# Two-layer attention and feed-forward decode step with gradients: order of the last pass's end, its last weight gradient and its last stores

## Chip, cores and metric

The kernel runs on one NeuronCore of a Trainium2 chip. The metric is the device time of one execution in microseconds; lower is better. The kernel before took 2014.3 us in the median of 8 runs (2004.38 to 2015.78).

## What is computed

One token passes twice through the same attention and feed-forward weights. The outputs are the result and the gradients of all inputs, among them those of the whole K and V caches (4 key/value heads, 65536 positions, 128 wide, 64 MB each in bf16), which are used by both layers, so that their gradients are sums over two layers.

```python
def _A_ref(x, k_cache, v_cache, wq, wo):          # 32 query heads, 4 key/value heads
    q = (x @ wq) ...
    scores = jnp.einsum("bhqd,bhkd->bhqk", q, k) * (Dh ** -0.5)
    p = _softmax(scores, axis=-1)
    o = jnp.einsum("bhqk,bhkd->bhqd", p, v)
    return o ... @ wo
...
x = x + _A_ref(_layernorm(x), A_k_cache, A_v_cache, A_wq, A_wo)
x = x + _B_ref(_layernorm(x), B_w1, B_b1, B_w2, B_b2)     # relu, squared
x = x + _A_ref(_layernorm(x), A_k_cache, A_v_cache, A_wq, A_wo)
x = x + _B_ref(_layernorm(x), B_w1, B_b1, B_w2, B_b2)
...
_out, _vjp = jax.vjp(_f, A_x, A_k_cache, A_v_cache, A_wq, A_wo, B_w1, B_b1, B_w2, B_b2)
_grads = _vjp(grad_out)
```

## The kernel before

The caches are streamed four times: two forward passes (one a layer), a backward pass for the second layer, and a last pass, `attn_bwd4` (L1192), that finishes the first layer's backward and writes the gradients dK and dV of both layers. K and V come in blocks of 1 MB (`J` = 32 columns of 128 positions); a group is one of the four key/value heads and has 16 blocks of each. In the last pass the groups run from 3 down to 0 and the blocks of a group from 15 down to 0, so group 0's block 0 is the last.

An item is a quarter of a block (8 columns). `pipeline` (L795) walks over the items; each stage is a function with a lag, and step i runs it on item i minus the lag:

- `vT` (lag 0): loads the V block where it is new and turns 8 tiles on TensorE (L1249); a copy brings them to SBUF (`kt`).
- `vS` (lag 2): 8 small products into `ps_sc` (L1282), and once a block the VectorE multiplication that makes `X` (L1290), dS of both layers; X is turned into `xt` (L1262).
- `dV8` (lag 3): in the first two quarters of a block, `outer16` (L1295): four matmuls in row pairs into `ps_gg` (L1303) and two copies into a 1 MB staging slot. After the second call GpSimd issues the slot's store (L1309).
- `k8` (lag `B4_LAG` = 7): loads the K block where it is new, 8 matmuls into dQ's sum (`ps_acc`, L1329), and in the last two quarters `outer16` for dK, from the same `xt`. At the end of a group dQ is folded and `on_group` is called.

The copies (`evac`, L139) go to ScalarE (L150) or VectorE (L153), whichever has the smaller planned load.

All 1 MB pieces live in one arena of 20 slots (12, and 8 that hold the probabilities until a group is done). `take_one` (L268) picks a slot by the step in which it was given back: for a load the newest that is 9 steps old, for staging the newest that is 1 step old; a slot with a store counts as given back 5 steps later (`STORE_STEPS`, L67). Loads are issued by SyncE in program order (L331 for K and V, L425 for weights), stores by GpSimd in program order; an instruction waits on semaphores for what was last in its slot, so a late store holds up what comes next into its slot. GpSimd also makes `xin`, a copy of probabilities that X's block needs (L1256).

Between the stages a background list runs the other gradients, a piece a step: the outer products for w1, w2, wo and wq (`g_outer`, L1371), and the products that give dn and dO. A wq gradient of one group is 2 MB: `rows2` (L1345) turns two vectors into rows (`rowb` from dQ, `rowa` from the layer norm's output, twice), `rank2` (L1362) makes eight pieces of 128 x 1024 that are copied, and two stores of 1 MB go out (L1386). The one for the last group runs after the pass:

```python
    attn_bwd4(3, L1, L3, on4, bg, b4, [(12 + B4_LAG, last_v), (12, pre_load("wq4", lambda: wq_slabs(lastg[3], 2))), (5, fill4)])
    bg.drain()
    run(gwq(lastg[3]))
```

The list at the end gives functions with the number of steps before the pass's end in which they run: the last three V loads, the loads of the last wq slabs, and `fill4`, which turns the wq slabs (64 transposes, L637). When the last dQ is folded, `on4` (L1621) runs the product with these slabs (`PRE["rows"].run()`, L669), the layer norm's backward, and stores dx0 (L193). The instructions' order on each engine is that of a list scheduler within the dependencies, not always that of the source.

Of the kernel before, what the change touches and what calls it, by code (L numbers as in the profile page):

```python
# [20 lines left out]
def kernel(  # L21
# [117 lines left out]
    def evac(out, in_, kind="bf"):  # L139
        n = 1  # L140
        for d in in_.shape[1:]:
            n *= d
        ca = 0.17 + n * 0.00083
        cd = 0.13 + n * (0.00105 if kind == "f32" else 0.00054)

        if PS["pass4"] and kind == "bf":
            ca += 1.5
        if kind == "kta" or kind != "kt" and load["act"] + ca <= load["dve"] + cd:
            load["act"] += 0.17 + n * 0.00083
            nc.scalar.copy(out=out, in_=in_)  # L150
        else:
            load["dve"] += cd
            nc.vector.tensor_copy(out=out, in_=in_)  # L153
# [12 lines left out]
    def col_from_dram_f(v1d, n, name):  # L166
        nj = n // P
        rows = tmp.tile([nj // 4, 4 * P], BF, name="rows_f", tag="rows_f", bufs=1)
        nc.sync.dma_start(out=rows[:], in_=v1d.rearrange("(s x) -> s x", x=4 * P))
        pt = ps_mv([P, 4, 8], BF)  # L170
        col = vec.tile([P, nj // 4, 4], F32, name=name)
        for j in range(4):
            nc.tensor.transpose(pt[:, j, 0:nj // 4], f_cols(rows, j), ident_b[0:nj // 4, 0:nj // 4])
            nc.vector.tensor_copy(out=col[:, :, j], in_=pt[:, j, 0:nj // 4])
        return col[:, :, :].rearrange("p s j -> p (s j)")

    def col_to_dram_f(col, n, v1d):
        nj = n // P
        rows = tmp.tile([nj // 4, P, 4], BF, name="rows_f", tag="rows_f", bufs=1)
# [5 lines left out]
        nc.gpsimd.dma_start(out=v1d.rearrange("(s x) -> s x", x=4 * P), in_=rows[:].rearrange("s p j -> s (p j)"))  # L185
# [191 lines left out]
    B4_LAG = TLEAD + J // 8 + 1  # L377
# [814 lines left out]
    def attn_bwd4(p, La, Lb, on_group, bg, stack, end=()):  # L1192
# [16 lines left out]
        def g_setup(g):  # L1209
# [6 lines left out]
            ndt = dspool.tile([64, J, R2], BF, name="ndt4", tag="ndt4", bufs=1)  # L1216
            for i, L in enumerate((La, Lb)):
                nc.vector.tensor_copy(out=ndt[:, :, i * R:(i + 1) * R], in_=L["nd2"][:, sl].unsqueeze(1).to_broadcast([64, J, R]))
# [48 lines left out]
        def vS(g, c8):  # L1267
# [27 lines left out]
        def outer16(name, out, key, xt, gg, j1):  # L1295
# [4 lines left out]
            for m in range(2):  # L1300
# [6 lines left out]
                evac(stg[:, jj:jj + 8, :].rearrange("p j d -> p (j d)"), pg[:, :], kind="f32")  # L1307
            if j1 + 16 == J:
                nc.gpsimd.dma_start(out=out, in_=stg)  # L1309
                state.pop(key).free(stored=True)  # L1310

        def dV8(g, c8):
            b, j0 = divmod(c8, J)
            if 2 * j0 < J:
                outer16("gstv", half(GVv, g, b), "stv", state[("xe", g, b)], state[("GG", g, c8 // SU)][1], 2 * j0)

        def k8(g, c8):
# [3 lines left out]
            X, xt = state[("xd", g, b)]  # L1321
# [40 lines left out]
    def rank2(out, lhs, rhs):  # L1362
# [6 lines left out]
        evac(out, pg[:, 0:n], kind="f32")  # L1369

# [250 lines left out]
    def on4(g):  # L1621
# [54 lines left out]
```

## Time and profile before

| stretch of the profiled execution | length us | TensorE busy | granted clock | DMA share | GB/s |
|---|---|---|---|---|---|
| start of the last pass, 1212 to 1310 | 98.0 | 78.60 | 0.81 | 0.78 | 298 |
| its body, 1310 to 1900 | 590.0 | 494.07 | 0.88 | 1.00 | 411 |
| 1900 to 1940 | 40.0 | 32.65 | 0.91 | 0.98 | 407 |
| 1940 to 1980 | 40.0 | 38.58 | 0.96 | 0.94 | 350 |
| 1980 to the end | 33.5 | 18.26 | 0.73 | 0.43 | 173 |

The profiled execution took 2015.27 us; its span on the core is 2013.5 us. Over the whole span TensorE is busy 80%, VectorE 58%, ScalarE 52%, and 794.97 MB move at 393 to 395 GB/s. Times in the views count from the start of the span. A DMA share of 1.00 means that all 16 DMA engines have packets in work all the time; the busy time of TensorE is modelled and does not mean its peak. In a timeline or a table of groups, the bracket at the end of a row is the idle time of that engine just before, and what ended it.

### The profile page before, as it was taken

The page shows a single profiled execution, that of the slowest core. Times are in us where ns is not written, and L with a number is a line of the kernel's source. Part 1 is how long each engine was busy: PE and PEld are TensorE (multiplying, and loading weights), DVE is VectorE, ACT ScalarE, POOL GpSimd, SP SyncE. Part 2 cuts the span into 40 slices and gives each one's busy share as a digit, 9 for nine tenths or more (in the row PEclk, how much of TensorE's full clock was granted, in tenths as well). Part 3 has the DMA queues.
Part 4 walks back from the last instruction along what each step waited for, and adds up shares of the span by engine and source line. Part 5 has one row for each costly group of instructions (what it writes and reads, how often), then busy time and mean ns, then how long its engine had stood idle before and what let it go on. Part 6 is the DMA issues. An engine that isn't in the chain of part 4 may idle for free. (4 is left out here: it accounts for less than half of the span.)

```text
span 2013.5 us, 67001 instructions
## 1 busy us (share of the span) xinstructions
PE 1607.8 (80%) x30210; PEld 1310.0 (65%) x30210; DVE 1174.5 (58%) x2358; ACT 1043.9 (52%) x1613; POOL 143.4 (7%) x332
## 2 busy tenths in 40 slices
PE   6877788687777786877777887888878878698986
PEld 6877777587777686767777785455545555455554
DVE  5645455255545543545454466677758767678775
ACT  3444344253443353425363455577658667567665
POOL 0000000000000000000000001111112111111211
PEclk9989899799999997998898998789879989889888
DMA  9999999999999998999999986999999999999996
GB/s 389 421 419 419 419 422 404 395 402 419 419 418 420 420 403 298 363 420 420 421 416 410 402 301 256 346 423 424 421 411 414 403 423 383 368 422 425 423 369 241
DMA packets 110845, 794.97 MB, mean 395 GB/s; under 512 B 9424, under 2 KB 9438, under 8 KB 49374
## 3 DMA queue, kind: packets, MB, share of 16 engines
q1 hardware_dynamic: 86510, 624.99, 76.2%
q0 software_dynamic: 24048, 165.70, 19.9%
q8 instruction: 236, 3.87, 0.8%
q14 instruction: 51, 0.42, 0.1%
HBM read 624.96 MB, written 165.69 MB: 393 GB/s over the span
## 5 line engine op out<-in xcount | busy, mean ns | idle before, releaser
L153 DVE COPY kt<-ps_tr 128x1024 bf16<-128x1024 bf16 x724 | 497.6, 689 | 477.0 <-PE ps_tr L936 254.9
L150 ACT CAST arena<-ps_gg 128x1024 bf16<-128x1024 f32 x452 | 440.2, 1010 | 223.3 <-PE ps_gg L1303 172.3
L936 PE MATMUL ps_tr<-ident_b,arena 128*128 128x128 bf16 x3840 | 310.2, 226 | 59.5 <-DMA arena<-in_A_k_cache_dram 39.7
L936 PEld LDWEIGHTS <-arena 128*128 128x128 bf16 x3840 | 234.4, 101 | 64.1 <-DMA arena<-in_A_k_cache_dram 41.1
L153 DVE CAST arena<-ps_gg 128x1024 bf16<-128x1024 f32 (+1 forms) x191 | 228.8, 1198 | 79.1 <-PE ps_gg L1303 40.0
L150 ACT COPY kt<-ps_tr 128x1024 bf16<-128x1024 bf16 x164 | 172.4, 1053 | 192.4 <-PE ps_tr L1128 126.5
L1303 PE MATMUL ps_gg<-GG,xt 64*128 64x512 bf16 x1024 | 214.1, 416 | 43.6 <-DVE arena L153 25.7
L1038 PE MATMUL ps_acc<-arena 128*128 128x64 bf16 (+4 forms) x4096 | 204.3, 195 | 50.6 <-DMA arena<-in_A_v_cache_dram 32.6
L1249 PE MATMUL ps_tr<-ident_b,arena 128*128 128x128 bf16 x1824 | 178.2, 235 | 44.1 <-DMA arena<-in_A_v_cache_dram 43.1
L954 PE MATMUL ps_sc<-L_qpad,kt 128*128 128x64 bf16 (+7 forms) x3584 | 183.6, 194 | 19.5 <-issue 14.3
L1128 PE MATMUL ps_tr<-ident_b,arena 128*128 128x128 bf16 x1920 | 156.2, 227 | 50.4 <-DMA arena<-in_A_v_cache_dram 49.0
L1019 ACT ACTIVATE arena<-S_sb,L_negm 128x128 bf16<-128x128 f32 x256 | 165.6, 1003 | 55.1 <-DVE L_negm L1004 55.1
L1038 PEld LDWEIGHTS <-arena 128*128 128x128 bf16 x4096 | 158.2, 100 | 53.2 <-DMA arena<-in_A_v_cache_dram 35.0
L1249 PEld LDWEIGHTS <-arena 128*128 128x128 bf16 x1824 | 120.4, 105 | 99.1 <-issue 51.6
L954 PEld LDWEIGHTS <-kt 128*128 128x128 bf16 x3584 | 153.2, 100 | 26.4 <-issue 19.7
L1128 PEld LDWEIGHTS <-arena 128*128 128x128 bf16 x1920 | 118.3, 102 | 54.0 <-DMA arena<-in_A_v_cache_dram 52.2
L1329 PE MATMUL ps_acc<-X,arena 128*128 128x64 bf16 (+3 forms) x2048 | 119.5, 198 | 15.7 <-DMA arena<-in_A_k_cache_dram 15.7
L1019 ACT ACTIVATION_READ_ACCUMULATOR arena<-S_sb,L_negm 128x1 f32 x256 | 128.1, 500 | 0.0
L1329 PEld LDWEIGHTS <-arena 128*128 128x128 bf16 x2048 | 86.7, 102 | 51.6 <-issue 34.1
L1282 PE MATMUL ps_sc<-DOB,kt 128*128 128x64 bf16 (+3 forms) x1824 | 118.0, 200 | 0.0
L1282 PEld LDWEIGHTS <-kt 128*128 128x128 bf16 x1824 | 86.0, 103 | 47.9 <-issue 46.4
L1173 PE MATMUL ps_acc<-dsT,arena 128*128 128x64 bf16 (+7 forms) x2048 | 102.8, 194 | 16.8 <-DMA arena<-in_A_k_cache_dram 12.3
(269 smaller groups left out, 2099.9 us busy)
## 6 DMA issues: line engine op xcount, KB each, us to landing
arena<-in_A_k_cache_dram SPq DMA_DIRECT2D x86, 2048.0 KB, 20.7
arena<-in_A_v_cache_dram SPq DMA_DIRECT2D x83, 2048.0 KB, 21.8
out_dram<-arena POOLq DMA_DIRECT2D x151, 1024.0 KB, 11.2
arena<-in_A_v_cache_dram SPq DMA_DIRECT2D x76, 1024.0 KB, 15.2
arena<-in_A_k_cache_dram SPq DMA_DIRECT2D x76, 1024.0 KB, 12.8
arena<-in_B_w_dram SPq DMA_DIRECT2D x32, 896.0 KB, 6.9
arena<-in_A_wq_dram SPq DMA_DIRECT2D x22, 1024.0 KB, 14.0
arena<-in_A_wo_dram SPq DMA_DIRECT2D x18, 1024.0 KB, 15.9
```

The lines of the kernel that those rows point to most:

```text
L150: nc.scalar.copy(out=out, in_=in_)
L153: nc.vector.tensor_copy(out=out, in_=in_)
L936: nc.tensor.transpose(pt[:, i, :], kb8[:, i, :], ident_b[:, :])
L954: nc.tensor.matmul(state["ps_s"][:, s:s + w, :].rearrange("p a b -> p (a b)"), lhsT=kt[:, i, :], rhs=L["qpad"][:, g, 0:w, :].rearrange("p ...
L1019: nc.scalar.activation(out=E(p, g, c0, SU)[:, :, h], in_=S[:, h, :], func=ACTF.Exp, bias=L["negm"][:, g, su, h:h + 1], scale=SCALE, accum_ ...
L1038: nc.tensor.matmul(ps_o[:, 0:w, :], lhsT=vb8[:, i, :], rhs=E(p, g, c, w), start=(c % SU == 0), stop=(c % SU == SU - 1), skip_group_check=True)
L1128: nc.tensor.transpose(pt[:, i, :], vb8[:, i, :], ident_b[:, :])
L1173: nc.tensor.matmul(ps_dq[:, 0:w, :].rearrange("p a b -> p (a b)"), lhsT=kb8[:, i, :], rhs=dsT[:, s:s + w, :].rearrange("p a b -> p (a b)") ...
L1249: nc.tensor.transpose(pt[:, i, :], vb8[:, i, :], ident_b[:, :])
L1282: nc.tensor.matmul(state["ps_dp"][:, s:s + w, :].rearrange("p a b -> p (a b)"), lhsT=vt[:, i, :], rhs=DOB[:, g, 0:w, :].rearrange("p a b - ...
L1303: nc.tensor.matmul(pg[:, 512 * h:512 * h + 512], lhsT=xt[64 * h:64 * h + 64, j1 // 8 + m, :], rhs=gg[64 * h:64 * h + 64, :, :].rearrange(" ...
L1329: nc.tensor.matmul(ps_dq[:, 0:w, :].rearrange("p a b -> p (a b)"), lhsT=kb8[:, i, :], rhs=X[:, s:s + w, :].rearrange("p a b -> p (a b)"), ...
```

## The change

In six parts (a few lines of the helpers `col_from_dram_f` and `col_to_dram_f`, which take the arena slot, are left out of the diff):

- dK gets a stage of its own, `dK8`, at the old lag of 7 (`DK_LAG`); `k8`, now dQ alone, runs four items later (`B4_LAG` = 11), and so K blocks are asked for one block later. X gets a third buffer, the rows `ndt` shrink from 32 copies to one that is broadcast, and `rows_f` becomes an arena slot.
- A finished staging slot is put in a list (`pend`). Its store is issued when the list is longer than `held` allows: nothing is held before item 24 of the last group (of 64), then one, two from item 32, three from item 40. `cap` lets them go 7, 5 and 3 steps before the end.
- Each store also waits for the copy that was recorded last when the store is recorded (`add_manual_dep`).
- The last group's wq gradient, `g_outer_last`: both `rowa` are made in `fill4`, `rowb` as soon as dQ is folded, then one `rank2` after the product for dn and the other seven after the dx0 store; four stores of 0.5 MB.
- The remaining background work is drained in `fill4` rather than after the pass.
- The wq slabs are loaded 20 steps before the pass's end instead of 12, and `fill4` runs 10 steps before it instead of 5; the pass is four steps longer.

```diff
@@
             ca += 1.5
         if kind == "kta" or kind != "kt" and load["act"] + ca <= load["dve"] + cd:
             load["act"] += 0.17 + n * 0.00083
-            nc.scalar.copy(out=out, in_=in_)
-        else:
-            load["dve"] += cd
-            nc.vector.tensor_copy(out=out, in_=in_)
+            return nc.scalar.copy(out=out, in_=in_)
+        load["dve"] += cd
+        return nc.vector.tensor_copy(out=out, in_=in_)
 
 
     def col_from_dram(v1d, n, name):
...
@@
 
     FWD_LAG = TLEAD + SU // 8 + 18
     B3_LAG = TLEAD + HB // 8 + 3
-    B4_LAG = TLEAD + J // 8 + 1
+    DK_LAG = TLEAD + J // 8 + 1
+    B4_LAG = DK_LAG + J // 8
     DV_LAG = TLEAD + 1
     ITEMS = [order_by_unit(False, SU), order_by_unit(True, SU), order_by_unit(False, HB), order_by_unit(True, J)]
     TOUCH = [touch_order(ITEMS[0], [("k", 0), ("v", FWD_LAG)]), touch_order(ITEMS[1], [("k", 0), ("v", FWD_LAG)]),
@@
                 nc.vector.scalar_tensor_tensor(out=CCf[:, g, 0, i * R:(i + 1) * R], in0=L["qT"][:, sl], scalar=SCALE, in1=L["rZ"][:, sl],
                                                op0=ALU.mult, op1=ALU.mult)
                 nc.vector.tensor_tensor(out=CCf[:, g, 1, i * R:(i + 1) * R], in0=L["dOT"][:, sl], in1=L["rZ"][:, sl], op=ALU.mult)
-            ndt = dspool.tile([64, J, R2], BF, name="ndt4", tag="ndt4", bufs=1)
+            ndt = dspool.tile([64, R2], BF, name="ndt4", tag="ndt4")
             for i, L in enumerate((La, Lb)):
-                nc.vector.tensor_copy(out=ndt[:, :, i * R:(i + 1) * R], in_=L["nd2"][:, sl].unsqueeze(1).to_broadcast([64, J, R]))
+                nc.vector.tensor_copy(out=ndt[:, i * R:(i + 1) * R], in_=L["nd2"][:, sl])
             state["ndt"] = ndt
 
         def su_setup(g, su):
@@
                 if s == 0:
                     state["ps_dp"] = ps_sc([P, J, R2])
                     nc.tensor.matmul(state["ps_dp"][:, :, :].rearrange("p c r -> p (c r)"), lhsT=sel2[:, :],
-                                     rhs=state["ndt"][:, :, :].rearrange("o c r -> o (c r)"), start=True, stop=False)
+                                     rhs=state["ndt"][:, :].unsqueeze(1).to_broadcast([64, J, R2]), start=True, stop=False)
                 w = min(4, J - s)
                 nc.tensor.matmul(state["ps_dp"][:, s:s + w, :].rearrange("p a b -> p (a b)"), lhsT=vt[:, i, :],
                                  rhs=DOB[:, g, 0:w, :].rearrange("p a b -> p (a b)"), start=False, stop=(s == J - 1))
@@
             if (c8 + 8) % J == 0:
                 c0 = c8 + 8 - J
                 ps_dp = state["ps_dp"]
-                X = dspool.tile([P, J, R2], BF, name="X", tag="X")
+                X = dspool.tile([P, J, R2], BF, name="X", tag="X", bufs=3)
                 nc.vector.tensor_tensor(out=split2(X[:, :, :]), in0=split2(ps_dp[:, :, :]), in1=E2(g, c0, J), op=ALU.mult)
                 add_load(dve=0.13 + J * R2 * 0.00105)
                 state[("xd", g, c0 // J)] = (X, x_transpose(X[:, :, :]))
                 E_done(g, c0, J)
 
-        def outer16(name, out, key, xt, gg, j1):
+        place = {k: i for i, k in enumerate(items)}
+        n_g = len(items) // G
+        pend = deque()
+
+        def store(ins):
+            out, stg, sl = pend.popleft()
+            st = nc.gpsimd.dma_start(out=out, in_=stg)
+            tc.add_manual_dep(st.ins, ins.ins.name, mybir.DependencyInfo(mybir.DependencyClass.Sync, mybir.DependencyReason.DATA),
+                              reason="stores follow the loads of later blocks")
+            sl.free(stored=True)
+
+        def held(g, c8):
+
+            i = place[(g, c8)] - (len(items) - n_g)
+            return min(sum(8 * i >= k * n_g for k in (3, 4, 5)), state.get("cap", 3))
+
+        def cap(n):
+            def f():
+                state["cap"] = n
+                while len(pend) > n:
+                    store(state["evac"])
+            return f
+
+        def outer16(name, g, c8, out, key, xt, gg, j1):
 
             if j1 == 0:
                 state[key] = Slot(name, True)
@@
                                      rhs=gg[64 * h:64 * h + 64, :, :].rearrange("p a b -> p (a b)"),
                                      start=True, stop=True, tile_position=(64 * h, 0))
                 jj = j1 + 8 * m
-                evac(stg[:, jj:jj + 8, :].rearrange("p j d -> p (j d)"), pg[:, :], kind="f32")
+                state["evac"] = evac(stg[:, jj:jj + 8, :].rearrange("p j d -> p (j d)"), pg[:, :], kind="f32")
             if j1 + 16 == J:
-                nc.gpsimd.dma_start(out=out, in_=stg)
-                state.pop(key).free(stored=True)
+                pend.append((out, stg, state.pop(key)))
+                while len(pend) > held(g, c8):
+                    store(state["evac"])
 
         def dV8(g, c8):
             b, j0 = divmod(c8, J)
             if 2 * j0 < J:
-                outer16("gstv", half(GVv, g, b), "stv", state[("xe", g, b)], state[("GG", g, c8 // SU)][1], 2 * j0)
+                outer16("gstv", g, c8, half(GVv, g, b), "stv", state[("xe", g, b)], state[("GG", g, c8 // SU)][1], 2 * j0)
+
+        def dK8(g, c8):
+            b, j0 = divmod(c8, J)
+            if 2 * j0 >= J:
+                outer16("gstk", g, c8, half(GKv, g, b), "stk", state[("xd", g, b)][1], state[("GG", g, c8 // SU)][0], 2 * j0 - J)
 
         def k8(g, c8):
             kb8 = kv8("k", g, c8)
             b, j0 = divmod(c8, J)
             su = c8 // SU
-            X, xt = state[("xd", g, b)]
+            X = state[("xd", g, b)][0]
             if c8 == sufirst[(g, su)]:
                 state["ps_dq"] = ps_acc([P, 4, R2])
             ps_dq = state["ps_dq"]
@@
                 fold_dq(La, g, su, ps_dq[:, 0, 0:R], gfirst[g] // SU == su, glast[g] // SU == su, dspool)
                 if glast[g] // SU == su:
                     on_group(g)
-            if 2 * j0 >= J:
-                outer16("gstk", half(GKv, g, b), "stk", xt, state[("GG", g, su)][0], 2 * j0 - J)
 
         start_pass(p)
-        pipeline(items, [(vT, 0), (vS, TLEAD), (dV8, DV_LAG), (k8, B4_LAG)], bg, end)
+        pipeline(items, [(vT, 0), (vS, TLEAD), (dV8, DV_LAG), (dK8, DK_LAG), (k8, B4_LAG)], bg,
+                 list(end) + [(3 + 2 * n, cap(n)) for n in range(3)])
 
 
 
@@
             r = slice(64 * h, 64 * h + 2)
             nc.tensor.matmul(pg[:, 512 * h:512 * h + 512], lhsT=lhs(r), rhs=rhs(r), start=True, stop=True, tile_position=(64 * h, 0))
         evac(out, pg[:, 0:n], kind="f32")
+
+    def g_outer_last(pool, out_dram, a_cols, b_cols, c0):
+
+        ras = []
+        for a0 in (0, 4):
+            ra = pool.tile([66, 4 * P], BF, name="rowa", tag="rowa", bufs=2)
+            rows2(a_cols, (a0, a0), ra)
+            ras.append(ra)
+        sls = [Slot("og", True) for _ in ras]
+        yield
+        rb = pool.tile([66, 4 * P], BF, name="rowb", tag="rowb")
+        rows2(b_cols, (0, 4), rb)
+        yield
+        for a, (ra, sl) in enumerate(zip(ras, sls)):
+            og = sl.t[:, :].rearrange("p (j n) -> p j n", j=4)
+            rows = out_dram[a * 512:(a + 1) * 512, c0:c0 + 1024].rearrange("(p j) n -> p j n", j=4)
+            for j in range(4):
+                rank2(og[:, j, :], lambda r: f_cols(ra[r, :], j), lambda r: rb[r, :])
+                if j % 2:
+                    nc.gpsimd.dma_start(out=rows[:, j - 1:j + 1, :], in_=og[:, j - 1:j + 1, :])
+                yield
+            sl.free(stored=True)
 
     def g_outer(pool, out_dram, nA, nB, a_cols, b_cols, c0=0, a_f=False):
 
@@
             bg.add(g_dn(L1, dn1, g, g == firstg[3]))
             bg.normal.append(gwq(g))
         else:
+            next(PRE["gwq"])
             PRE["rows"].run()
+            next(PRE["gwq"])
             dxn1 = ln_bwd(dn1[:], L1["n"], L1["rstd"])
             dx0 = tmp.tile([P, DC], F32, name="dx0")
             nc.vector.tensor_tensor(out=dx0[:], in0=dx1[:], in1=dxn1[:], op=ALU.add)
             col_to_dram(dx0, D, out_1.rearrange("a b d -> (a b d)"))
+            run(PRE["gwq"])
 
     def last_v():
 
@@
         PRE["rows"] = Rows()
         PRE["rows"].add(PRE["wq4"], DC, R, lambda: L1["dqT"][:, gsl(lastg[3])], dn_finish(dn1, False))
         PRE["rows"].fill()
-    attn_bwd4(3, L1, L3, on4, bg, b4, [(12 + B4_LAG, last_v), (12, pre_load("wq4", lambda: wq_slabs(lastg[3], 2))), (5, fill4)])
-    bg.drain()
-    run(gwq(lastg[3]))
+        bg.drain()
+        PRE["gwq"] = g_outer_last(bgpool, out_4, [L3["n"], L1["n"]], [L3["dqT"][:, gsl(lastg[3])], L1["dqT"][:, gsl(lastg[3])]],
+                                  lastg[3] * 1024)
+        next(PRE["gwq"])
+    attn_bwd4(3, L1, L3, on4, bg, b4, [(12 + B4_LAG, last_v), (20, pre_load("wq4", lambda: wq_slabs(lastg[3], 2))), (10, fill4)])
     b4.close()
     ps4_stack.close()
 
```

More of the change, by code (lines that the diff above doesn't have):

```diff
@@ L167, in col_from_dram_f @@
         nj = n // P
-        rows = tmp.tile([nj // 4, 4 * P], BF, name="rows_f", tag="rows_f", bufs=1)
-        nc.sync.dma_start(out=rows[:], in_=v1d.rearrange("(s x) -> s x", x=4 * P))
+        sl = Slot("rows_f")
+        rows = sl.t[0:nj // 4, 0:4 * P]
+        nc.sync.dma_start(out=rows, in_=v1d.rearrange("(s x) -> s x", x=4 * P))
         pt = ps_mv([P, 4, 8], BF)
@@ L174, in col_from_dram_f @@
             nc.vector.tensor_copy(out=col[:, :, j], in_=pt[:, j, 0:nj // 4])
+        sl.free()
         return col[:, :, :].rearrange("p s j -> p (s j)")
@@ L178, in col_to_dram_f @@
         nj = n // P
-        rows = tmp.tile([nj // 4, P, 4], BF, name="rows_f", tag="rows_f", bufs=1)
+        sl = Slot("rows_f", True)
+        rows = sl.t[0:nj // 4, 0:4 * P].rearrange("s (p j) -> s p j", j=4)
         c3 = col[:, :].rearrange("p (s j) -> p s j", j=4)
@@ L184, in col_to_dram_f @@
             nc.vector.tensor_copy(out=rows[:, :, j], in_=pt[:])
-        nc.gpsimd.dma_start(out=v1d.rearrange("(s x) -> s x", x=4 * P), in_=rows[:].rearrange("s p j -> s (p j)"))
+        nc.gpsimd.dma_start(out=v1d.rearrange("(s x) -> s x", x=4 * P), in_=sl.t[0:nj // 4, 0:4 * P])
+        sl.free(stored=True)
     def col_to_dram(col, n, v1d):
@@ L1369, in rank2 @@
         evac(out, pg[:, 0:n], kind="f32")
+    def g_outer_last(pool, out_dram, a_cols, b_cols, c0):
[17 more added lines that the diff above has]
+                yield
+            sl.free(stored=True)
     def g_outer(pool, out_dram, nA, nB, a_cols, b_cols, c0=0, a_f=False):
```

## The prediction

> **What bounds the kernel now.** I read the 40 slices first, then short windows over the end of the last pass, then its waits, then the timelines of VectorE and GpSimd and the chain that ended last.
>
> ```profile
> DMA  9999999999999998999999986999999999999996
> GB/s 389 421 419 419 419 422 404 395 402 419 419 418 420 420 403 298 363 420 420 421 416 410 402 301 256 346 423 424 421 411 414 403 423 383 368 422 425 423 369 241
> ```
>
> The page: the sixteen DMA engines are busy to nine tenths almost everywhere, at some 420 GB/s. What is lost in the last pass (from 1212 us on) lies at its start (256 and 346) and in the last two slices (369 and 241). The change works on the end.
>
> ```profile
> core 0: us, PE busy (x) PEld busy (x) DVE busy (x) ACT busy (x) POOL busy (x), PEclk, DMA share, GB/s
> ...
> 1880.00:1890.00 10.00, 10.00 (x84) 5.51 (x83) 6.18 (x8) 4.98 (x5) 0.82 (x2) 0.50 1.01 424
> ...
> 1920.00:1930.00 10.00, 7.55 (x102) 4.92 (x99) 5.25 (x12) 6.40 (x8) 1.81 (x3) 1.00 1.01 417
> 1930.00:1940.00 10.00, 6.56 (x62) 3.36 (x61) 5.56 (x6) 4.26 (x5) 1.15 (x2) 0.66 0.87 364
> ...
> 1975.00:1980.00 5.00, 4.67 (x70) 3.04 (x68) 3.59 (x5) 3.57 (x4) 0.55 (x1) 1.00 1.00 405
> 1985.00:1990.00 5.00, 4.08 (x61) 2.83 (x61) 2.70 (x9) 3.67 (x4) 0.36 (x1) 1.00 0.51 210
> 1990.00:1995.00 5.00, 3.36 (x75) 2.52 (x71) 2.83 (x12) 1.24 (x3) 0.53 (x1) 1.00 0.05 20
> 2005.00:2013.50 8.50, 0.00 (x0) 0.00 (x0) 0.29 (x1) 0.00 (x0) 0.72 (x1) 0.50 0.32 123
> ```
>
> Windows (length, busy time of each engine, granted TensorE clock, DMA share, GB/s): DMA is full until 1930, nearly so until 1980, and almost empty in 1990 to 1995. So up to about 1930 the time is bytes; from there it is TensorE's work and the hand-over between engines. TensorE is busy 4.67 of 5 us just before 1980, so those blocks cannot run much faster by data that come sooner.
>
> ```profile
> DVE mv_t L553 <- DMA arena<-in_A_wo_dram: 13.0, 1, 13.0
> DVE arena L153 <- DMA out_dram<-arena: 4.3, 1, 4.3
> ...
> 1926.15 0.69 DVE L153 COPY kt<-ps_tr 128x1024 bf16<-128x1024 bf16 x1 [0.32 <-PE ps_tr L1249]
> 1931.16 1.22 DVE L153 CAST arena<-ps_gg 128x1024 bf16<-128x1024 f32 x1 [4.32 <-DMA out_dram<-arena]
> ```
>
> Waits (us in total, times, longest) and the VectorE timeline: a copy into a staging slot stood 4.32 us because the store that had been in that slot, issued at 1910.49 by the chain, landed at 1931.1, 20.6 us later. The copies to X (L1290), one a block, follow each other by 17.5 us here (1921.68, 1939.22); the next three gaps are 10.5, 10.8 and 11.0. This block lost 7.0 us.
>
> ```profile
> 1989.60 2.10 PE ps_acc L669 x64
> 1992.05 1.22 DVE arena L153
> 1993.44 0.70 DVE rowb L153
> 1994.99 0.70 DVE rowa L153
> ...
> 1999.82 0.58 ACT rowa L150
> ...
> 2004.06 1.24 DVE arena L153
> 2005.82 0.74 POOLq L1671
> ```
>
> The chain: after the last X at 1978.5 it goes through the product for dn (L669), the last dK copy, the rows of the last wq gradient (two `rowa`, one `rowb`), eight rank-2 copies, and one store of 1 MB, issued at 2005.85, which lands at the end of the span, 7.65 us later.
>
> **The change, part by part.** The profiled execution took 2015.27 us, its span 2013.5, so 1.77 lies around it. It is 1.0 above the median of the eight runs (2014.3); I sum against the execution and take 1.0 off at the end.
>
> *Stores held in the last group, and K loads asked for one block later.* By the time the pass is some ten blocks from its end, up to 3 MB of stores and 1 MB of K load no longer stand among the transfers that a block's V load and slot must wait for. Upper end: 4 x 1.05 MB at 420 GB/s = 10.0 us. Lower end: the loads come no earlier (they wait for slots, not bandwidth) and the hold is worth only what it does to the 4.32 us wait. In the built order of the changed kernel the like copy stands 300 instructions behind its store, not 392; a block is some 300 instructions in 10.7 us, so that is 10.7 us. Three fewer MB (7.5 us) bring the landing from 20.6 to 13.1: 2.4 of wait remain out of 4.3, which in proportion of the 7.0 us leaves a gain of 3.1. Between 3.1 and 10.0 I take the middle, **-6.5**; the nearest row, the 7.0 us, lies there.
>
> *The load wait before it.* TensorE waited 1.83 us for a V load at 1879.10, and its clock was 0.50 in 1880 to 1890; that block's gap was 14.1 instead of 10.5. The K load that now comes a block later (2.5 us) covers the wait: 0 to -3.6. I take the bare wait, **-1.8**, since the clock may fall for another reason.
>
> [...]
>
> *A late weight load.* In the changed order the second half of a wq slab lands in a slot that X's reads also cover: X of the fifth block of the group waits for a load released only one block (240 instructions, 8.6 us) before. A 1 MB wq load takes 14.0 us in the median (page, last line): 5.4 us of wait. Like the 13.0 us wait of L553, during which DMA stayed at 1.01 to 1.03 and then fell to 0.65 for 10 us (3.5 us lost), it costs what DMA loses: 3.5 x 5.4/13.0 = **+1.5**, between 0 and 5.4. The cover is the bytes still owed; without it all 5.4 count.
>
> *Start of the pass.* The order has one K load issued ahead of the pass instead of two, where DMA was 0.61, 0.20 and 0.64 busy (1210 to 1240): up to +2.5. But TensorE's 7.4 us wait for K at 1249.62 now falls four items later: down to -7.4. DMA is short of work there either way: **0**.
>
> *The tail after the last X.* Off the path go `rowa` twice (1.55 us from the end of `rowb` to the next matmul, and 1.33 at 1999.1), and one rank-2 copy (1.0) overlaps L669: -3.9. Sixteen small transposes (two eights of 0.40) and four ACT casts of 0.58 now stand before the last dQ: 0.8 to 2.3, I take +1.6. dQ of the last block, 32 matmuls (four eights of 0.37), comes behind the dK copies, which it used to precede: same work, 0. The last store is then ready some 2.3 us earlier. On GpSimd's queue, however, the four half stores stand behind the store of dx0, which waits for the layer-norm chain: L669's end to that store took 6.8 us (1991.7 to 1998.51). With L669 ending at about 1995.3 it issues at 2002.1, and the halves from 2002.6 at 0.53 to 0.72 each, the last at 2004.5, 1.3 earlier than 2005.85. The transfers: 2.1 MB at 420 GB/s take 5.0 us; the old last store took 7.65, of which 2.5 are its bytes. End: 2002.6 + 5.15 + 5.0 = 2012.7, against 2013.5: -0.8. If the dx0 store doesn't delay them: -2.3 and half of 2.5, -3.6, so the bounds are -3.6 and +1.5 (no gain, all casts in the way). I take the half-way of -0.8 and -2.0 (rows ready sooner than I count), **-1.4**.
>
> [...]
>
> *Without price.* The small `ndt` (two copies a group shrink) and X's third buffer lie beside full DMA; without that cover they are under 1 us a group.
>
> Sum: 2015.27 - 6.5 - 1.8 + 1.5 + 0 - 1.4 = 2007.1; less 1.0: **2006**.
>
> **The rivals.** *Nothing to measure* (1.0 within 0.3%, about what a measurement here can tell): loads are not brought forward. For it: SyncE's queue waited 60.6 us on landed stores after 1900, so a load is gated by a slot, which held stores free later. Only the tail is left: 2015.27 - 1.4 - 1.0 = 2012.9.
>
> *Slower: slots.* Three held stores keep three of twenty slots, so staging slots come back sooner after their store: 300 instructions at the place above, and 296 (10.6 us) for the last block's dK copies behind the store of a dV. If stores still take up to 20.6 us, the first wait is 9.9 instead of 4.3 (+5.6) and the second 0.6 to 10 (+5.3), at a time when TensorE has no slack: 2015.27 + 10.9 - 1.4 - 1.0 = 2023.8. It decides once a store in the last group takes more than some 13 us. Against it: the stores issued after 1885 landed in 9.6 us in the median.
>
> *Faster than forecast*: the full 10.0, and halves not delayed (-3.6): 2015.27 - 13.6 - 1.0 = 2000.7.
>
> **How the numbers follow.** Forecast 0.46 (nearly all below 2008.3), faster still 0.13, nothing to measure 0.19, slots 0.22. Faster by over 0.3%: 0.57; within: 0.21; slower: 0.22. The forecast's own range is 2001 to 2012; to hold eight in ten it must reach into both neighbours: 1996 to 2021.
>
> **What would show it.** Right: no VectorE wait on a store over 3 us after 1900; X of the last block before 1973; DMA over 0.9 busy to the end but for 5 us; the chain's last 25 us without `rowa`. Wrong: X copies still 11 us and more apart from 1870 on, a wait on `arena` for a store of 8 us or more, or the four halves issued after 2004. Large differences before 1800 would make the prediction wrong by another cause.

## The result and the profile after

The changed kernel took 2024.73 us in the median of 11 runs (2020.32 to 2031.07), beside 2012.7 for the kernel before in the same series: a ratio of 1.0064, 95% interval 1.0050 to 1.0078. It is slower, where 2006 was forecast. Its profiled execution took 2017.16 us, 1.9 more than that of the kernel before; it is faster than every one of the 11 timed runs, so the views below show only a part of the loss, and the sizes of the parts are taken from timed runs. A second profile of the same kernel took 2021.13 us.

The 40 slices of the changed kernel: DMA share and GB/s.

```profile
DMA  9999999999999998999999986999999999899987
GB/s 390 420 419 420 420 421 405 391 396 419 418 419 419 420 406 314 378 419 421 417 415 414 394 321 247 373 406 422 423 418 422 397 402 397 358 421 414 372 335 295
```

The start of the last pass (321, 247) is about as it was, but the last three slices now move 372, 335 and 295 GB/s, where the kernel before had 423, 369 and 241: bytes have moved from the last blocks into the end. Windows over the last group of the changed kernel, columns as before:

```profile
1830.00:1840.00 10.00, 8.83 (x150) 6.16 (x147) 9.15 (x16) 9.02 (x14) 1.90 (x4) 1.00 1.01 422
1840.00:1850.00 10.00, 1.79 (x15) 0.79 (x14) 0.46 (x1) 1.37 (x2) 0.00 (x0) 0.69 1.02 427
1850.00:1860.00 10.00, 0.43 (x4) 0.34 (x4) 1.18 (x2) 0.00 (x0) 0.61 (x1) 0.50 1.02 415
1860.00:1870.00 10.00, 10.00 (x85) 5.29 (x84) 7.30 (x15) 7.13 (x10) 1.61 (x3) 0.62 0.85 340
1870.00:1900.00 30.00, 28.08 (x400) 18.45 (x400) 27.08 (x47) 24.57 (x29) 8.10 (x14) 1.00 1.00 386
1900.00:1940.00 40.00, 36.21 (x505) 23.38 (x503) 31.73 (x57) 29.99 (x33) 5.97 (x10) 0.99 0.94 352
1940.00:1980.00 40.00, 37.88 (x445) 23.03 (x446) 29.01 (x54) 28.82 (x32) 7.73 (x13) 0.84 0.87 332
1980.00:2015.40 35.40, 19.86 (x267) 11.81 (x265) 17.58 (x34) 15.56 (x18) 6.56 (x11) 0.79 0.67 268
```

Between 1840 and 1860 TensorE does 2.22 us of work in 20, with DMA full: everything waits for one transfer. From 1870 on TensorE is busy 94, 91 and 95% of the time while DMA falls to 352 and 332 GB/s, so by these shares the pace there is TensorE's, and from 1900 on DMA has room that is not used. What VectorE waited for between 1690 and 1990 in the changed kernel (us in total, times, longest):

```profile
DVE X L1294 <- DMA arena<-in_A_wq_dram: 18.4, 1, 18.4
...
DVE X L1294 <- DMA arena<-in_A_wo_dram: 16.3, 1, 16.3
...
DVE arena L152 <- DMA out_dram<-arena: 1.2, 1, 1.2
```

SyncE's timeline there, and VectorE's (start, us, instruction):

```profile
1836.10 0.88 SPq L334 DMA_DIRECT2D arena<-in_A_k_cache_dram  x2
1837.08 0.43 SPq L429 DMA_DIRECT2D arena<-in_A_wq_dram  x1
```

```profile
1832.25 0.68 DVE L1294 TENSOR_TENSOR X<-ps_sc,arena 128x512 bf16<-128x512 f32 x1
...
1858.82 0.69 DVE L1294 TENSOR_TENSOR X<-ps_sc,arena 128x512 bf16<-128x512 f32 x1 [18.37 <-DMA arena<-in_A_wq_dram]
```

X (L1294 here) reads the probabilities of both layers as one range of the arena, and that range covers slots of finished groups that lie between its two planes. A half of a weight slab was put into such a slot. The load must wait for the X before (1832.25), the next X waits for the load, though it uses none of its data, and VectorE's queue stands behind it. There are two such waits: a wq half in the last group, and a wo half a group earlier (near 1720). GpSimd's `xin` waited 19.6 us for a wq half as well. The wait on a store that the prediction started from is gone (1.2 us left).

The X copies show where the ground was won and lost. In the kernel before, X number 40 of 64 (counted from 0) stood at 1706.00, in the changed kernel at 1692.12: 13.9 us ahead. At number 53 it is 1860.35 against 1873.84, 13.5 behind; at the last one 1978.49 against 1981.10. Of the 13.9 us, 6.0 are there at the first X already (1222.48 against 1216.49); over all the profiles of this series the first X stands between 1215.71 and 1224.32, so these 6.0 are no gain that can be told from scatter. So the early part of the pass gained at most some 8 us, blocks 41 to 53 lost 27 us, and the last ten took 107.3 us instead of 118.1; by its busy share TensorE is what limits them.

The end, by GpSimd's timeline of the changed kernel (L1305 the held stores, L196 dx0, L1421 the halves):

```profile
1994.79 1.58 POOL L1305 DMA_DIRECT2D out_dram<-arena  x3 [2.59 <-DVE arena L152]
2004.08 0.53 POOL L196 DMA_DIRECT2D out_dram<-rows_c  x1 [7.71 <-DVE rows_c L195]
2004.61 2.87 POOL L1421 DMA_DIRECT2D out_dram<-arena  x4
```

From the last X to the end of the span it is 34.3 us, where it was 35.0. In the second profile of the changed kernel it is 36.1.

### The profile page after: what moved, and what is told of

Same layout as the page of the kernel before. It is cut to its first block, busy times and chain, and to the rows that moved or that the text cites. A ratio compares the mean times of both kernels' runs of the same rounds, so it can differ in the third digit from the quotient of the medians.

```text
span 2015.4 us, 66960 instructions
## 1 busy us (share of the span) xinstructions
PE 1606.6 (80%) x30210; PEld 1311.3 (65%) x30210; DVE 1170.2 (58%) x2357; ACT 1044.9 (52%) x1614; POOL 145.6 (7%) x334
## 5 line engine op out<-in xcount | busy, mean ns | idle before, releaser
L152 DVE CAST arena<-ps_gg 128x1024 bf16<-128x1024 f32 (+2 forms) x191 | 228.3, 1195 | 81.9 <-PE ps_gg L1330 43.3
L958 PE MATMUL ps_sc<-L_qpad,kt 128*128 128x64 bf16 (+7 forms) x3584 | 182.9, 194 | 19.7 <-issue 13.2
L1253 PE MATMUL ps_tr<-ident_b,arena 128*128 128x128 bf16 x1824 | 177.2, 233 | 10.8 <-DMA arena<-in_A_v_cache_dram 10.2
L1362 PE MATMUL ps_acc<-X,arena 128*128 128x64 bf16 (+3 forms) x2048 | 116.2, 200 | 56.1 <-DMA arena<-in_A_k_cache_dram 56.1
L1177 PE MATMUL ps_acc<-dsT,arena 128*128 128x64 bf16 (+7 forms) x2048 | 104.9, 196 | 16.6 <-DMA arena<-in_A_k_cache_dram 11.4
L1286 PE MATMUL ps_sc<-DOB,kt 128*128 128x64 bf16 (+3 forms) x1824 | 113.6, 199 | 0.0
## 6 DMA issues: line engine op xcount, KB each, us to landing
arena<-in_A_k_cache_dram SPq DMA_DIRECT2D x76, 1024.0 KB, 13.2
arena<-in_A_wq_dram SPq DMA_DIRECT2D x22, 1024.0 KB, 17.4
```

Of the source, the lines that this page charges most:

```text
L152: return nc.vector.tensor_copy(out=out, in_=in_)
L958: nc.tensor.matmul(state["ps_s"][:, s:s + w, :].rearrange("p a b -> p (a b)"), lhsT=kt[:, i, :], rhs=L["qpad"][:, g, 0:w, :].rearrange("p ...
L1177: nc.tensor.matmul(ps_dq[:, 0:w, :].rearrange("p a b -> p (a b)"), lhsT=kb8[:, i, :], rhs=dsT[:, s:s + w, :].rearrange("p a b -> p (a b)") ...
L1253: nc.tensor.transpose(pt[:, i, :], vb8[:, i, :], ident_b[:, :])
L1286: nc.tensor.matmul(state["ps_dp"][:, s:s + w, :].rearrange("p a b -> p (a b)"), lhsT=vt[:, i, :], rhs=DOB[:, g, 0:w, :].rearrange("p a b - ...
L1362: nc.tensor.matmul(ps_dq[:, 0:w, :].rearrange("p a b -> p (a b)"), lhsT=kb8[:, i, :], rhs=X[:, s:s + w, :].rearrange("p a b -> p (a b)"), ...
```

## The experiments

Three theories. Theory 1: the late weight loads make the loss. Theory 2: the held stores do, since their bytes lie at the end. Theory 3: dQ's lag of four items does. Each kernel was timed against the kernel before on its own chip, so ratios are compared; 0.001 is 2 us. The tool for theory 1 is one rule in `take_one`, called "the rule" below, which keeps weight loads of the last pass out of the slots that hold probabilities or lie between them:

```diff
         else:
+            if PS["pass4"]:
+                by_age = [x for x in by_age if x[1] < NSLOT] or by_age
             i = by_age[0][1]
```

### The rule, and with it no held stores or no lag

The kernel before with the rule:

> The kernel before, with one rule added: in the last pass a weight load takes the oldest slot that holds no E plane, so no X and no xin waits for a weight load. Theory 1 (the late weight loads make the loss: X and xin wait for a load that a slot of a finished group releases late): the kernel before has one such wait, GpSimd's xin on a half of wo, and its V and K waits stay, so 2009 to 2013 us, a ratio of 0.998 to 1.000. Theory 2 (the held stores make it) and theory 3 (dQ four items behind dK makes it) say nothing here beyond 0.998 to 1.002. Above 1.003 would mean that the slots which the rule gives instead are reused too soon, and the rule is then no clean tool.

2008.41 us, ratio 0.9980 (0.9967 to 0.9993): the lower edge of what theory 1 said, and all three theories allow it. It is not above 1.003, so the rule serves as a tool.

The changed kernel with the rule:

> The changed kernel with the same rule: the two waits of X on weight loads (16.3 and 18.4 us in its profile) and the one of xin (19.6 us) must be gone from the list of waits. Theory 1: most of the loss goes, 2010 to 2016 us, a ratio to the kernel before of 0.999 to 1.002. Theory 2: the loss stays, 2021 to 2026 us, ratio 1.004 to 1.007, because the bytes of the held stores still lie at the end. Theory 3: it stays too, with the K waits at 56 us or more.

2007.85 us, ratio 0.9977 (0.9968 to 0.9987), lower than any theory had it: 0.0087, 17 us, come off. The waits of X are gone from the list. In VectorE's waits of this run, over the same blocks, the longest on a transfer is a store's (ScalarE's copies waited 9.6 us on two stores, where they had waited 1.7 without the rule, so its slots are not free of waits either):

```profile
DVE arena L152 <- DMA out_dram<-arena: 3.7, 1, 3.7
```

No held stores (`held` returns 0), with the rule:

```diff
-            return min(sum(8 * i >= k * n_g for k in (3, 4, 5)), state.get("cap", 3))
+            return 0
```

> The changed kernel with the rule, and no store held back in the last group. Theory 1: as with the rule alone within 3 us, 2010 to 2016 us, or up to 6 us more if the held stores earn what the prediction gave them. Theory 2: 7 to 12 us less than with the rule alone, about 2012 us, a ratio of 0.999 to 1.001. Theory 3: as with the rule alone.

2002.42 us, ratio 0.9952 (0.9937 to 0.9967): 5 us less than with the rule alone.

No lag, with the rule:

```diff
-    B4_LAG = DK_LAG + J // 8
+    B4_LAG = DK_LAG
...
-    ... (20, pre_load("wq4", ...)), (10, fill4)])
+    ... (16, pre_load("wq4", ...)), (6, fill4)])
```

> The changed kernel with the rule, and dQ back in the same item as dK, with the preload of the last weight halves and the fill four items earlier, as they then stand to the stages; the held stores stay. Theory 1: as with the rule alone within 3 us. Theory 2: no better than with the rule alone, 2021 to 2026 us. Theory 3: 7 to 12 us less than with the rule alone, about 2012 us, with the K waits back from 56 us to about 16 and the V waits up again to about 43.

1996.64 us, ratio 0.9921 (0.9905 to 0.9937): 11 us less than with the rule alone. So with the rule in place, undoing the held stores or the lag brings more, and the question is how the parts add.

### Which load, and each part alone

The rule for wq halves alone (`Slot` hands its name to `take_one`, and the rule asks for `name == "s_wq"`):

> The changed kernel with the rule for the wq halves alone: the late wq half of the last group (18.4 us of X's wait) is gone, the late wo half a group earlier (16.3 us) stays as it was. If the two waits share the 17 us that the rule brought (2024.7 to 2007.9), this stands at 2013 to 2019 us. If the last one alone makes the loss, since what the pass loses earlier it makes up behind full DMA, it stands at 2007 to 2011 us; if the earlier one alone does, at 2021 us or more.

2015.99 us, ratio 1.0017 (1.0001 to 1.0033): the wo load alone costs 8 us over the full rule.

The rule for wo halves alone (`name == "s_wo"`):

> The changed kernel with the rule for the wo halves alone. The wo load is early; the two wq halves of the last group now both fall into plane slots, released 285 and 292 instructions before an X or xin needs them (240 in the changed kernel, 285 for xin in the kernel before). If the price goes by whether a load falls into a plane slot at all, 8 to 10 us above the kernel with the full rule, 2015 to 2018 us. If it goes by the distance, so that 45 instructions more (some 2 us of TensorE) hide most of it, 2008 to 2012 us.

2021.49 us, ratio 1.0041 (1.0021 to 1.0060): 13 us over the full rule. The distance didn't help; xin waited 29.3 us in two pieces for the wq halves in this run, the longer 25.5, and X 14.9.

No lag, without the rule:

> The changed kernel without the rule, dQ back in dK's item, with the preload of the last weight halves and the fill four items earlier: this part of the change alone undone. The weight loads then fall where those of the kernel before fall: of the three waits of X and xin only xin's 285 instructions behind the release is left. Theory 1 with the measured price of that wait (3 to 4 us, the kernel before with the rule) and the run with rule and lag undone (1996.6): 1999 to 2002 us, a ratio of 0.993 to 0.996. If the late loads came with the held stores or the last gradient rather than with the lag, it would stay above 2010 us.

2013.03 us, ratio 0.9991 (0.9973 to 1.0009): a miss, 11 to 14 us above the 1999 to 2002 expected. Only the late wo load is left here, but X is not what waits for it. VectorE's waits of this run:

```profile
DVE mv_t L557 <- DMA arena<-in_A_wo_dram: 17.7, 1, 17.7
```

The weight product's own multiplication, which truly needs the load, stands in VectorE's queue and holds it as long: VectorE was ready for it at 1707.64, and it went on at 1725.34. The covered range is one way to be caught by a load that lands late (X waited 18.4 us in the changed kernel); a reader that heads its engine's queue is another (17.7 us here). When this load was issued, and what it stood behind, is not shown.

No held stores, without the rule:

> The changed kernel without the rule and with no store held back: this part alone undone, the two late weight loads and dQ's four items stay. If the held stores cost the same here as with the rule (5.4 us), 2018 to 2021 us, a ratio of 1.002 to 1.005. If they are what makes the late loads wait long (fewer bytes in flight, later slots), the loss goes nearly whole: 2010 to 2015 us. If they earn what the prediction gave them once X waits anyway, 2025 to 2031 us.

2009.60 us, ratio 0.9988 (0.9975 to 1.0000). Both late loads are still there (15.5 and 15.4 us of X's wait), and nearly the whole loss is gone.

Rule, no lag, no held stores:

> Rule, no held stores, no lag: what is left of the change is the last wq gradient prepared and stored in halves. If the costs of lag (11.2 us) and held stores (5.4 us, measured with the lag) add up, 1990 to 1993 us. If the held stores cost only because the lagged dQ pushes the end past them, or if they earn what the prediction gave them, 1996 to 2003 us.

1999.66 us, ratio 0.9933 (0.9914 to 0.9952): the parts don't add.

No rule, no lag, no held stores:

> No rule, no lag, no held stores: the late wo load of the kernel before (xin 285 instructions behind the release) and the last gradient in halves. If the late load costs what it costs the kernel before (4 us) and the gradient brings its 9 us, 2001 to 2005 us, a ratio of 0.995 to 0.997. If the late load costs as much as with held stores and no lag (14 to 16 us), 2011 to 2016 us.

2006.73 us, ratio 0.9978 (0.9963 to 0.9992), between its two ranges; the multiplication of the weight product waits 13.4 us for wo here. The changed kernel once more, in the same series:

> The changed kernel once more, beside the others on one chip. A ratio of 1.005 to 1.008 as before, 2021 to 2027 us, if the corner is sound; below 1.003 would mean that the parts add better than the runs so far say.

2026.59 us, ratio 1.0080 (1.0055 to 1.0104). The ratios together:

| weight loads | lag and held stores | lag alone | held stores alone | neither |
|---|---|---|---|---|
| as placed | 1.0064, 1.0080 | 0.9988 | 0.9991 | 0.9978 |
| with the rule | 0.9977 | 0.9952 | 0.9921 | 0.9933 |

(Without the lag only the wo load is late, with it the wo and a wq load.) The rule is worth 7 and 9 us where nothing is held (0.9988 to 0.9952, 0.9978 to 0.9933) and 14 to 21 where stores are held (0.9991 to 0.9921, 1.0064 and 1.0080 to 0.9977). Held stores cost 15 and 18 us in the changed kernel (its two series), 5 with the rule, and without the lag they do nothing clear of the intervals (0.9978 to 0.9991 as placed, 0.9933 to 0.9921 with the rule). So most of the loss is the meeting of held stores with late loads and lag: undoing any one of them takes some 15 to 21 us off (the lag takes the late wq load with it).

### The store of dx0

The store of dx0 issued by SyncE, with the rule:

```diff
-            col_to_dram(dx0, D, out_1.rearrange("a b d -> (a b d)"))
+            col_to_dram(dx0, D, out_1.rearrange("a b d -> (a b d)"), nc.sync)
```

> Rule, lag and held stores as in the changed kernel, and the store of dx0 issued by SyncE. With the rule alone GpSimd waited 9.26 us for dx0 and then issued the four half stores back to back in 2.87 us, the last 10.1 us before the end. If that queue sets the end, the first three halves go out 3 to 6 us sooner and the end comes 2 to 5 us sooner: 2003 to 2006 us. If the bytes that the held stores leave set it, less than 1.5 us: 2006.5 to 2009 us.

2007.95 us, ratio 0.9991 (0.9981 to 1.0001): nothing. And without the lag, with and without held stores:

> Rule, no lag, stores held, and the 4-KB store of dx0 issued by SyncE, so that GpSimd's four stores of the last gradient's halves don't queue behind its 5.5-us wait for the end of the layer norm. If that queue sets the end, the first halves go out some 3 us sooner and the end comes 1 to 3 us earlier than without it (1996.6): 1993.5 to 1995.5 us. If the last half's own evacuation sets the end (its store was issued 1 us after the third in the run without), no difference: 1995.5 to 1998 us.

1996.31 us, ratio 0.9911 (0.9895 to 0.9927).

> Rule, no lag, no held stores, dx0 by SyncE: beside the same with held stores (1996.3) it tells once more what the held stores do without the lag. Where they earn 2.4 us, as the pair without SyncE's store had it (1999.7 against 1996.6), 1998 to 2000 us; where that was noise, 1995 to 1997.5 us; where they earn the 6.5 us of the prediction, 2001 to 2004 us.

2000.94 us, ratio 0.9953 (0.9937 to 0.9970). The queue behind dx0 doesn't set the end. Against 0.9911 the held stores earn 8 us in this pair by the ratios (4.6 by the medians), against 2 in the first: between them lies the best that they do.

### Release, number and bytes of the held stores

The release is counted from the end of the pipeline, which the lag moves four items. Released four items earlier (7, 9 and 11 steps before the end instead of 3, 5 and 7):

```diff
-                 list(end) + [(3 + 2 * n, cap(n)) for n in range(3)])
+                 list(end) + [(7 + 2 * n, cap(n)) for n in range(3)])
```

> The changed kernel with the held stores released four items earlier, that is as far behind the last X as without the lag; nothing else is touched. If the late release is what makes lag and held stores meet, half or more of the 15 us that no held stores bring: 2009 to 2017 us. If it is the stores held from the sixth block on, behind the stall of the late loads, less than 4 us: 2020 to 2026 us.

2020.66 us, ratio 1.0056 (1.0037 to 1.0076).

> The same with the rule. No held stores brought 2.5 to 5.4 us here, most of it in the tail (35.7 us from the last X to the end with them, 31.7 without). If the late release is the cause, 2002 to 2005 us with a tail of 32 to 33 us; if not, 2006 to 2009 us with a tail above 34.5 us.

2007.63 us, ratio 0.9983 (0.9969 to 0.9998), 34.2 us from the last X to the end. The first differs from the changed kernel within the intervals, the second not at all from the kernel with the rule. The time of the release is not it; this theory falls.

One store held instead of three (the value of `held` capped at 1), late loads and lag as in the changed kernel:

> The changed kernel with at most one store held in the last group instead of three; late loads and lag stay. If the price goes with the bytes held, a third of 15 us above the kernel that holds nothing: 2013 to 2016 us. If one held store is enough (the first begins at the sixth block, close behind the stall), 2019 us or more; if only the third one hurts, 2008 to 2012 us.

2013.76 us, ratio 1.0015 (0.9999 to 1.0031): 0.0027, 5.4 us, above the kernel that holds nothing, a third of what three cost.

The changed kernel without the wait that the change adds to each store, so that the slots and SyncE's order stay as they are, and the bytes go early (three halves of the last gradient then go ahead of dx0 as well):

```diff
             st = nc.gpsimd.dma_start(out=out, in_=stg)
-            tc.add_manual_dep(st.ins, ins.ins.name, ...)
```

> The changed kernel without the added wait of each store on the copy recorded last. SyncE's order and every slot stay as in the changed kernel, the list of held stores too, but on GpSimd a store is issued once its own copies are done, the three halves of the last gradient ahead of dx0 with them. If the waiting bytes make the 15 us, it stands with the kernel that holds nothing: 2008 to 2014 us, ratio 0.998 to 1.001. If the slots that the list gives back later make it, it stays at 2020 to 2027 us.

2013.12 us, ratio 1.0002 (0.9986 to 1.0019): 12 to 16 us come off with both late loads in place (16.5 and 18.6 us of X's wait). Its windows:

```profile
1870.00:1900.00 30.00, 27.86 (x404) 18.42 (x401) 26.93 (x48) 24.42 (x29) 8.78 (x15) 1.00 1.00 391
1900.00:1940.00 40.00, 37.33 (x506) 23.42 (x500) 31.34 (x58) 30.18 (x33) 7.16 (x13) 0.96 1.01 418
1940.00:1980.00 40.00, 37.60 (x511) 23.85 (x509) 33.23 (x58) 31.05 (x35) 8.33 (x14) 1.00 0.94 359
1980.00:2007.60 27.60, 15.32 (x208) 8.94 (x207) 13.51 (x29) 12.95 (x16) 4.50 (x7) 0.80 0.52 209
```

X number 53 stands at 1874.05, as in the changed kernel (1873.84): the stall is the same. Then DMA moves 418 and 359 GB/s where it moved 352 and 332, the last ten blocks take 102.5 us instead of 107.3, and 31.1 instead of 34.3 us lie behind the last X. So the price comes with the waiting of the stores, not with the slots that the list assigns. That three halves go ahead of dx0 is not likely to be the reason: with the rule, moving dx0 out of their way brought nothing.

One thing more differs in these profiles: in 1940 to 1980 the granted clock is 0.84 in the changed kernel (0.80 in its second profile) and 1.00 here, and TensorE does 445 matrix instructions there (434) against 511, in the same busy time. With nothing held it is 0.96. Whether the waiting bytes bring the lower clock on, or the clock falls by itself and takes a part of the time, no run separates; with the rule and held stores it is 0.91 there with the lag and 1.00 without it.

## Why the prediction was wrong, step by step

**Held stores and the later K load, -6.5: this step failed, in sign.** It priced them by the state of the kernel before, in which transfers limit the last blocks up to about 1930. The same text then added a load that stalls the pass, and left that state unchanged. After the stall the last ten blocks are limited by TensorE, by its busy share (91 and 95%); DMA has room there, which stores can use (418 GB/s against 352 when they are let go), and the change takes up to 3 MB of them out and lands them behind the last block. Measured as a part of the change: 15 us lost (1.0064 against 0.9988), 5.4 for the first store. Letting the stores go, with both late loads and the lag in place, takes it off again (1.0002). The wait of 4.32 us on a store that the term stood on did vanish. The 10 us that were the upper end come near the truth only in the kernel without lag and late loads (2 to 8 us earned).

**A late weight load, +1.5, at most 5.4: mis-sized.** The dependency was the right one, X of the fifth block of the last group. The wait was put at 5.4 us, a load of 14.0 less a lead of 8.6; it measured 18.4. The load was issued at 1837.08, 4.2 us after the X that frees its slot had ended (1832.93), behind two K loads in SyncE's queue, and took 21.7 us until 1858.8. Its neighbours were as slow: in 1830 to 1860, with the DMA share at 1.01 to 1.02, the median K load took 18.0 us and V load 20.4, where the prediction had 14.0 from the median of the whole execution. X would have been ready at 1840.45, 7.5 after: 4.2 + 21.7 - 7.5 = 18.4. The second such load, of wo a group earlier (16.3 us), was not priced: the kernel before has a like wait of 13.0, which was taken as a given. And "costs what DMA loses" counted the 10 us after the wait; with held stores DMA lost from 1900 to 1980 too (352 and 332 GB/s), with the stores let go only from 1940 on (418 and 359). Together the two cost 17 us here, and 7 where no store is held.

**The load wait before it, -1.8: right, and taken back.** TensorE's waits for V in the last pass fell from 43.1 to 10.2 us in total, but those for K rose from 15.7 to 56.1. Before and after (us in total, times, longest):

```profile
PE ps_tr L1249 <- DMA arena<-in_A_v_cache_dram: 43.1, 10, 10.0
...
PE ps_acc L1329 <- DMA arena<-in_A_k_cache_dram: 15.7, 4, 7.6
```

```profile
PE ps_acc L1362 <- DMA arena<-in_A_k_cache_dram: 56.1, 10, 9.2
...
PE ps_tr L1253 <- DMA arena<-in_A_v_cache_dram: 10.2, 5, 4.0
```

The wait moved to the other load. The lag, which the prediction counted as a gain (the K load asked for later), at the start and in the tail, costs 4 us with the rule, within the intervals (0.9952 against 0.9933), and 11 with held stores too (0.9977 against 0.9921).

**Start of the pass, 0 (between -7.4 and +2.5): perhaps mis-sized; the profiles can't tell.** By X number 40 the profiled changed kernel is 13.9 us ahead, 7.9 if one counts from the first X; beside the run with the rule and without the lag (1698.61) it is 6.5. But two runs that differ only in the last group's stores stand 4.9 apart at that X (1699.14 and 1704.07). The blocks behind it give all of it back.

**The tail, -1.4, worked as -0.8: right in the first profile** (34.3 against 35.0), and the working with it: the product for dn ends 16.6 us behind the last X, where the working's 1995.3 means 16.8 (13.2 before). The halves go out at 2004.61 and not at 2002.6, since the last X is 2.6 later. The second profile has 36.1, still within the stated bounds. With the rule, the tail is 35.7 us with lag and held stores, 31.7 with nothing held, 29.7 without the lag, 29.1 without either, and 34.9 in the kernel before. So the new last gradient is worth 5 to 6 us, and lag and held bytes use it up. What storing in halves costs or brings by itself is not shown; no run separates the halves from the work that is prepared earlier. That dx0 delays the halves, which the working charged, costs nothing that runs can see.

**The rivals.** The slower one gave 2023.8, near the result, by slots reused too soon; after 1690 VectorE waited 1.2 us on a store and ScalarE 1.7, so the number was near for a wrong reason: luck. Of the signs of being wrong the halves after 2004 showed, the wait of 8 us on a store did not, and the X copies from 1870 on were 8.3 to 14.0 us apart, 10.7 in the mean. Of the signs of being right the VectorE wait came true; the last X before 1973 and DMA over 0.9 did not.

What the whole of the change would have been on clean ground: the same last gradient and held stores with dQ in its old place and weights in clean slots, 1996.64 us, ratio 0.9921, beats both kernels; with dx0 on SyncE 0.9911.

**Still open.** Between the changed kernel and the one that lets the bytes go the first profile shows 8 us, 4.8 in the last ten blocks and 3.2 behind the last X. The second profile shows 11.7 (2021.13 against 2009.39), 6.7 in the last ten blocks and 5.0 behind the last X, near the 12 to 16 of the timed runs; so that is where the loss lies. The runs don't tell why held bytes make the blocks themselves slower: loads that get their slots later, because the stores land later, would be one reason, the lower clock another, and neither is shown.

## What to carry to other kernels

A wait isn't worth what it lasts, but what the engine that limits the stretch behind it can still make up; so when a change adds a stall ahead of a stretch, ask anew what limits that stretch before pricing the rest of the change there. Here, transfers put off to the end earned something (2 to 8 us) only where no stall stood ahead of the blocks that they made way for, and cost 15 us and more where one did. A load into a slot that some reader's range covers is a wait of that reader: look at what frees the slot, what stands before the load in its queue, and how long transfers take at that place (here 21.7 us, against a median of 14.0 for wq loads over the execution of the kernel before, and 17.4 over that of the changed one).

## What the runs showed of the hardware

The granted clock stood at 0.50 not only after a wait (1850 to 1860 above, TensorE busy 0.43 of 10 us) but also in stretches that TensorE filled. The second profile of the changed kernel (the 5 us before such a stretch, and the stretch), and the run with the rule for wo halves alone:

```profile
1935.00:1940.00 5.00, 3.86 (x39) 1.91 (x36) 2.32 (x3) 3.52 (x4) 0.00 (x0) 0.70 1.00 353
1940.00:1950.00 10.00, 10.00 (x86) 5.71 (x85) 6.15 (x9) 4.71 (x6) 1.82 (x3) 0.50 0.78 319
```

```profile
1950.00:1960.00 10.00, 10.00 (x87) 5.35 (x85) 5.79 (x12) 5.73 (x7) 1.26 (x2) 0.50 0.48 193
```

By the profile, whose busy time is modelled, TensorE is busy in the whole 10 us at half its clock, and DMA moves 319 and 193 GB/s there, where it moved 348 and 361 in 1900 to 1940. In the kernel before, a like window (1880 to 1890) kept DMA at 424, and its block took 14.1 us all the same; what such a stretch costs, no run isolates. What brings it on is not shown either; in the 40 us before the first of these TensorE is busy 36.60 us, at a granted clock of 0.96. Last, a single profiled execution can lie outside all timed runs of its kernel (2017.16 against 2020.32 to 2031.07 here), so two profiles 2 us apart said little of a difference of 12.
